# Mean and variance of six blocks: column sums in groups of 32 on VectorE, one 16-column product each on TensorE

## Chip, cores and metric

The kernel runs on one core of a Trainium2 chip. The metric is the time of one execution in microseconds (us), as the median of several; lower is better.

## What is computed

Eight batches go through an attention between 512 tokens and 32 states (8 heads of 64), then both results, joined to 544 rows of 512 channels, go through a normalised feed-forward layer and a gated convolution. What matters here is the normalisation in the middle:

```python
mu = np.mean(x, axis=-1, keepdims=True)
var = np.mean((x - mu) ** 2, axis=-1, keepdims=True)
xn = (x - mu) / np.sqrt(var + 1e-06) * g_ln
ch = np.maximum(xn @ w_ch1, 0.0) @ w_ch2
return (x + ch).astype(np.float32)
```

x has 512 channels (DM), w_ch1 maps them to 2048 (DFF), w_ch2 maps them back. The mean and the variance are sums over channels, one number for each token.

## The kernel before

Activations lie channels on partitions, tokens along the free axis: a block is the 512 tokens of one batch, held as four tiles of 128x512. So a sum over channels is a sum over partitions, and one number per token is wanted on all 128 partitions.

Matrix products with fp32 accuracy are made from two halves (type F32R), high and low: `mm3` (lines 77, 78, 79) issues three products for one. `segment(b, ...)` runs the feed-forward layer of block b in 16 steps f. In each step TensorE makes h, the hidden tile (6 products of 512 columns, lines 77 to 79 into the PSUM tag `mm`, which has two buffers), ScalarE and VectorE turn h into the halves `hid` (lines 680 and 684), and TensorE adds the step before into four accumulators (`second`, 12 products into `acc0` to `acc3`). The order of TensorE's instructions is the order in which the program writes them (`manual_schedule`); all other engines run each its own queue, filled by a planner from priorities (`at_prio`, a smaller number goes first) and the planner's own estimate of times.

The mean of blocks 2 to 7 is worked out ahead of the activations, from the attention weights `aT`: `mean_terms` makes a tile t of 128x512 in step 10 of the block before (lines 359, 360), `halves_of` splits it in two (lines 318, 320), and `x1_mean`, called in step 1 behind the products of h, lets `column_total` (line 327) multiply both halves with a matrix of ones, 512 columns each. That puts the mean (with a minus sign) of every token on every partition, in a PSUM buffer of the tag `at`. Just ahead of h in this step stand `m_steps` (line 144, small products of tile form 64*32) and `x1_group` (line 347, form 32*64), whose four results are copied from the accumulators' buffers to `x1` by ScalarE and VectorE (lines 354, 352).

The variance is made by the generator `x1_var`: four adds of x1 and the mean (line 375), squares on ScalarE (376), three adds on GpSimd (378, 381), `halves_of` again, and three steps later, at the end of step 4, `rstd_of`: `column_total`, a transposition of the 128x512 result in groups of 32 (line 333), a scale and offset on one column of each group (line 335, 128x16) and a power of -0.5 on GpSimd (line 337). `rstd_row` (line 430) transposes that back to a row after step 15, when the accumulators are scaled and added to x1 (lines 711, 714).

`background(b)` runs x1_var and then `attention_steps(b + 1)`, one piece a step. The last piece but one, in step 12, is `sread` (line 304, 32 products of tile form 128*32 into a buffer of the tag `mm`, then a transposition on VectorE, line 308). Step 13 begins with `m_steps` of the next block.

`t2` is a ring of six 128x512 buffers that all these steps share. Blocks 0 and 1 use another path (`x1_steps`), which also calls `halves_of` and `rstd_of`.

Of the kernel before, what the change touches and what calls it, by code (L numbers as in the profile page):

```python
# [9 lines left out]
F32 = mybir.dt.float32  # L10
# [10 lines left out]
P = 128  # L21
# [20 lines left out]


@with_exitstack
def tile_kernel(ctx: ExitStack, tc: tile.TileContext, xT, xk, stT, sn, w1, w2, wval, wout, convw, gln, ident, out):
    nc = tc.nc
    main = ctx.enter_context(tc.tile_pool(name="main", bufs=1))
    ps_acc = ctx.enter_context(tc.tile_pool(name="ps_acc", bufs=1, space=PSUM))
# [6 lines left out]
    def sb(shape, dt, tag, bufs=1):  # L55
        cnt[0] += 1
        return main.tile(shape, dt, tag=tag, bufs=BUFS.get(tag, bufs), name=f"{tag}_{cnt[0]}")
# [5 lines left out]
    def at_ps(shape):  # L63
        return ps(ps_at, "at", shape)
# [4 lines left out]
    def small(shape, dt, tag):  # L69
        return sb(shape, dt, tag, 2)  # L70
# [10 lines left out]
    def at_prio(p):  # L81
        tc.cur_priority = p

    x2d = [dram.tile([P, KT, S], F32, name=f"x2d{b}") for b in range(B)]
    x1d = dram.tile([B, P, KT, NS], F32, name="x1d")
    ident_sb = sb([P, P], F32, "ident")
    g_sb = sb([P, KT, 1], F32, "g")
    cw_sb = sb([P, KT, TAPS], F32, "cw")
    nhalf = sb([P, S // 32], F32, "nhalf")
# [19 lines left out]
    def load_xk(b):  # L109
        xn = sb([P, 4, H, D], F32, "big")  # L110
        nc.sync.dma_start(out=xn, in_=xk[b])
        loads[b].append(xn)
# [183 lines left out]
    def sread(b):  # L296
        a2T = a2s.pop(b)
        xn = loads[b][3]
        sr = ps(ps_mm, "mm", [P, 2, D]) if b > 1 else at_ps([P, 2, D])
        for u in range(2):  # L300
            for c in range(4):
                for p in range(KT):
                    r = slice(32 * p, 32 * p + 32)
                    nc.tensor.matmul(
                        sr[r, u, :], lhsT=a2T[u][:, c, r], rhs=xn[:, c, 2 * p + u, :], start=(c == 0), stop=(c == 3)
                    )
        srs = t2([P, 4, 32])
        nc.vector.transpose(srs.rearrange("p t n -> p (t n)"), sr.rearrange("p u d -> p (u d)"))
        for p in range(KT):
            nc.sync.dma_start(  # L310
                out=x1d[b, :, p, :].rearrange("(t j) n -> j t n", j=32), in_=srs[32 * p:32 * p + 32]
            )
# [3 lines left out]
    def halves_of(x, n, scale=1.0):  # L316
        hi, lo = (sb([P, n], F32R, "t2") for _ in range(2))
        nc.scalar.activation(hi, x, AF.Copy, scale=scale)
        if scale == 1.0:
            nc.gpsimd.tensor_tensor(lo, x, hi.bitcast(F32), op=ALU.subtract)  # L320
        else:
            nc.vector.scalar_tensor_tensor(lo, x, scale, hi.bitcast(F32), op0=ALU.mult, op1=ALU.subtract)
        return hi, lo

    def column_total(out, hl):
        for i in range(2):
            nc.tensor.matmul(out, lhsT=ones.to_broadcast([P, P]), rhs=hl[i], start=i == 0, stop=i == 1)

    def rstd_of(key, hl, n):
        var = ps(ps_mm, "mm", [P, n]) if key < 2 else at_ps([P, n])  # L330
        column_total(var, hl)
        turned = t2([P, n // 32, 32])
        nc.vector.transpose(turned.rearrange("p g n -> p (g n)"), var)
        rstd = small([P, n // 32, 1], F32, "rstd")
        nc.vector.tensor_scalar(rstd, turned[:, :, :1], 1.0 / DM, 1e-6, op0=ALU.mult, op1=ALU.add)
        rv = rstd.rearrange("p c o -> p (c o)")
        nc.gpsimd.tensor_tensor(rv, rv, nhalf[:, :n // 32], op=ALU.pow)
        rstds[key] = rstd

    def x1_group(b):  # L340
        sn_raw, aT = coef[b][1], aTs[b]
        x1s[b] = x1 = sb([P, KT, S], F32, "x1")
        xp = [ps(ps_acc, f"acc{k}", [P, S]) for k in range(KT)]
        for k in range(KT):
            r = slice(32 * k, 32 * k + 32)
            for u in range(2):
                nc.tensor.matmul(
                    xp[k][64 * u:64 * u + 64, :], lhsT=sn_raw[r, u, :], rhs=aT[r, u, :], start=True, stop=True
                )
        for k in range(KT):  # L350
            if k % 2:
                nc.vector.tensor_copy(x1[:, k], xp[k])
            else:
                nc.scalar.copy(x1[:, k], xp[k])

    def mean_terms(b):
        sbn, aT = coef[b][2], aTs[b]
        t = t2([P, S])
        nc.scalar.activation(t, aT[:, 0], AF.Copy, scale=sbn[:, 0])
        nc.vector.scalar_tensor_tensor(t, aT[:, 1], sbn[:, 1], t, op0=ALU.mult, op1=ALU.add)  # L360
        terms[b] = halves_of(t, S)

    terms = {}

    def x1_mean(b):
        mus[b] = mu = at_ps([P, S])
        column_total(mu, terms.pop(b))

    mus = {}

    def x1_var(b):
        x1, mu, sqs = x1s[b], mus[b], []
        for k in range(KT):
            xc = t2([P, S])
            nc.vector.tensor_tensor(xc, x1[:, k], mu, op=ALU.add)
            nc.scalar.activation(xc, xc, AF.Square)
            if k % 2:
                nc.gpsimd.tensor_tensor(sqs[-1], sqs[-1], xc, op=ALU.add)
            else:
                sqs.append(xc)  # L380
        nc.gpsimd.tensor_tensor(sqs[0], sqs[0], sqs.pop(), op=ALU.add)
        hl = halves_of(sqs[0], S)
        yield
        yield
        yield
        rstd_of(b, hl, S)
        yield

    def x1_steps(b):
        _, sn_raw, _, sbhl = coef[b]  # L390
# [42 lines left out]
    def attention_steps(b):  # L433
        state_coefs(b)
        sc = [at_ps([P, S]) for _ in range(2)]
        scores(b, sc)
        softmax2_exp(b, sc)
        yield
        softmax1_max(b)
        yield  # L440
        softmax2_norm(b)
        yield
        softmax1_norm(b)
        yield
        softmax2_turn(b)
        yield
        softmax1_out(b)
        mean_terms(b)
        yield
        yield  # L450
        sread(b)
        yield
        if b + 1 < B:
            load_state(b + 1)
            load_x(b + 1)
            load_xk(b + 1)
# [3 lines left out]
    def sread_block_steps():  # L460
        xs = sb([P, KT, NTS], F32, "big")
        for k in range(KT):
            nc.sync.dma_start(out=xs[:, k].rearrange("p (b n) -> p b n", n=NS), in_=x1d[:, :, k, :].rearrange("b p n -> p b n"))
        yield
        t = t2([P, 2, NTS])
        nc.gpsimd.tensor_tensor(t, xs[:, :2], xs[:, 2:], op=ALU.add)
        nc.gpsimd.tensor_tensor(t[:, 0], t[:, 0], t[:, 1], op=ALU.add)
        hl = halves_of(t[:, 0], NTS, -1.0 / DM)
        yield
        yield  # L470
        mu = at_ps([P, NTS])
        column_total(mu, hl)
        xc = sb([P, KT, NTS], F32, "big")
        xn = sb([P, 2, KT, NTS], F32R, "ahl")
        for k in range(KT):
            nc.vector.tensor_tensor(xc[:, k], xs[:, k], mu, op=ALU.add)
        yield
        for k in range(KT):
            nc.scalar.activation(xn[:, 0, k], xc[:, k], AF.Copy, scale=g_sb[:, k])
            nc.vector.scalar_tensor_tensor(  # L480
                xn[:, 1, k], xc[:, k], g_sb[:, k], xn[:, 0, k].bitcast(F32), op0=ALU.mult, op1=ALU.subtract
            )
        xns[B] = xn
        x1s[B] = xs
        yield
        sq = [t2([P, 2, NTS]) for _ in range(2)]
        for i in range(2):
            nc.scalar.activation(sq[i], xc[:, 2 * i:2 * i + 2], AF.Square)
        nc.gpsimd.tensor_tensor(sq[0], sq[0], sq[1], op=ALU.add)
        nc.gpsimd.tensor_tensor(sq[0][:, 0], sq[0][:, 0], sq[0][:, 1], op=ALU.add)  # L490
        hl = halves_of(sq[0][:, 0], NTS)
        yield
        yield
        rstd_of(B, hl, NTS)
        yield

# [118 lines left out]
    def segment(b, f0, f1, n, nxt, bg):  # L615
        accs = {}
        for f in range(f0, f1):
# [24 lines left out]
                    split_w1(f // 2 + 1)  # L642
            if f == 1 and 1 < b < B:
                x1_group(b)
            at_prio(base)
            h = ps(ps_mm, "mm", [P, n])
            if b < B:
# [21 lines left out]
            if unit == (1, 0) and f % QF == 2:  # L669
                at_prio(base - 1500)  # L670
                m_steps(*unit)
            if f == 1 and 1 < b < B:
                x1_mean(b)
            if f == f1 - 1:
                at_prio(base + LATE)
                for _ in bg:
# [193 lines left out]
    for o in order[8:20]:  # L870
        load_tile(*o)
    load_xk(1)
    for o in order[24:26] + order[20:24]:
        load_tile(*o)
    late = order[26:]
# [77 lines left out]
    def background(b):  # L953
        yield
        if b == 3:
            val_weights.append(prep_weights(wval, wv, ["raw"] * KT))
        for i, _ in enumerate(x1_var(b)):
            if i == 2 and val_weights:
                next(val_weights[0], None)
            yield  # L960
        if b + 1 < B:
            yield from attention_steps(b + 1)
        else:
            yield
            yield from sread_block_steps()

    def before_phase_b():
# [115 lines left out]
```

## Time and profile before

| what | value |
|---|---|
| median of 3 runs | 890.83 us (890.58 to 890.91) |
| the profiled execution | 890.99 us |
| its span, first to last instruction | 889.2 us |
| mean granted TensorE clock | 0.996 |
| TensorE busy | 873.5 us, 98% of the span |
| VectorE, ScalarE, GpSimd busy | 571.8, 385.8, 210.3 us |

The profile page gives busy time by engine, by slice of the span and by source line; the trace behind it gives every instruction with its start and duration. A product's recorded duration includes the way through the array, so the distance between the starts of two products says what one costs, not its duration.

### The profile page before, as it was taken

The page shows a single profiled execution, that of the slowest core. Times are in us where ns is not written, and L with a number is a line of the kernel's source. Part 1 is how long each engine was busy: PE and PEld are TensorE (multiplying, and loading weights), DVE is VectorE, ACT ScalarE, POOL GpSimd, SP SyncE. Part 2 cuts the span into 40 slices and gives each one's busy share as a digit, 9 for nine tenths or more (in the row PEclk, how much of TensorE's full clock was granted, in tenths as well). Part 3 has the DMA queues.
Part 4 walks back from the last instruction along what each step waited for, and adds up shares of the span by engine and source line. Part 5 has one row for each costly group of instructions (what it writes and reads, how often), then busy time and mean ns, then how long its engine had stood idle before and what let it go on. Part 6 is the DMA issues. An engine that isn't in the chain of part 4 may idle for free.

```text
span 889.2 us, 12522 instructions
## 1 busy us (share of the span) xinstructions
PE 873.5 (98%) x4970; PEld 666.0 (75%) x4970; DVE 571.8 (64%) x957; ACT 385.8 (43%) x715; POOL 210.3 (24%) x172
## 2 busy tenths in 40 slices
PE   7997999999999999999999999999999999999998
PEld 2355767777777777777777777777899988888886
DVE  6899985666644553573464446243468799988870
ACT  4865744243433341443443235132337555455531
POOL 0001010013234321513522442162301124322100
PEclk8999999999999999999999999999999999999999
DMA  9932210121112101211120100110130212222112
GB/s 358 408 109 74 98 52 1 74 73 53 51 48 76 54 0 52 74 51 52 51 71 1 63 36 1 27 48 1 48 139 6 95 71 77 90 96 95 69 73 72
DMA packets 26667, 66.44 MB, mean 75 GB/s; under 512 B 10864, under 2 KB 13040, under 8 KB 22512
## 3 DMA queue, kind: packets, MB, share of 16 engines
q1 hardware_dynamic: 25984, 65.24, 20.4%
q8 instruction: 39, 0.64, 0.3%
q10 hardware_dynamic: 624, 0.40, 0.2%
q14 instruction: 20, 0.16, 0.1%
HBM read 47.80 MB, written 17.83 MB: 74 GB/s over the span
## 4 chain that ended last, share of the span: by engine, by line
PE 92%; DVE 4%; DMA 2%; ACT 1%; issue 1%; SPq 0%; DVEq 0%; ACTq 0%
PE acc L77 16%; PE acc L78 16%; PE acc L79 16%; PE mm L77 9%; PE mm L78 9%; PE mm L79 9%; PE at L144 2%; PE at L77 2%; PE at L79 2%; PE at L78 2%; PE mm L144 1%; PE mm L982 1%; DMA big<-in_xT 1%; PE mm L651 1%; PE acc L697 1%; PE at L287 1%
## 5 line engine op out<-in xcount | busy, mean ns | idle before, releaser
L77 PE MATMUL acc<-hid,w 128*128 128x512 f32 (+1 forms) x560 | 212.3, 379 | 0.1
L78 PE MATMUL acc<-hid,w 128*128 128x512 f32 (+1 forms) x560 | 211.4, 378 | 0.0
L79 PE MATMUL acc<-hid,w 128*128 128x512 f32 (+1 forms) x560 | 211.3, 377 | 0.0
L684 DVE SCALAR_TENSOR_TENSOR hid<-mm,hid 128x512 fp32r<-128x512 f32 (+1 forms) x140 | 91.8, 655 | 159.5 <-ACT hid L680 159.4
L680 ACT ACTIVATE hid<-mm 128x512 fp32r<-128x512 f32 (+2 forms) x144 | 82.2, 571 | 205.5 <-PE mm L79 204.1
L77 PE MATMUL mm<-ahl,m 128*128 128x512 f32 (+1 forms) x312 | 119.7, 384 | 3.4 <-DVE ahl L249 1.7
L77 PEld LDWEIGHTS acc<-hid,w 128*128 128x128 f32 x560 | 105.4, 188 | 23.0 <-issue 1.7
L79 PEld LDWEIGHTS acc<-hid,w 128*128 128x128 f32 x560 | 105.4, 188 | 19.8
L78 PEld LDWEIGHTS acc<-hid,w 128*128 128x128 f32 x560 | 105.4, 188 | 19.5
L78 PE MATMUL mm<-ahl,m 128*128 128x512 f32 (+1 forms) x312 | 115.3, 369 | 1.2 <-DVE m L74 1.2
L79 PE MATMUL mm<-ahl,m 128*128 128x512 f32 (+1 forms) x312 | 115.0, 369 | 0.0
L763 DVE SCALAR_TENSOR_TENSOR ahl<-big,cw,ahl 128x511 f32<-128x511 f32 (+3 forms) x128 | 102.2, 843 | 0.3
L74 POOL TENSOR_TENSOR m<-mb,m 128x512 fp32r<-128x512 f32 x48 | 61.4, 1299 | 123.0 <-ACT m L73 123.0
L73 ACT ACTIVATE m<-mb 128x512 fp32r<-128x512 f32 x62 | 38.7, 632 | 110.7 <-DVE mb L155 110.5
L77 PEld LDWEIGHTS mm<-ahl,m 128*128 128x128 f32 x312 | 58.8, 188 | 36.7 <-issue 12.1
L78 PEld LDWEIGHTS mm<-ahl,m 128*128 128x128 f32 x312 | 58.9, 189 | 11.3 <-DVE m L74 2.4
L79 PEld LDWEIGHTS mm<-ahl,m 128*128 128x128 f32 x312 | 58.8, 189 | 9.9
L749 POOL TENSOR_TENSOR w<-big,w 128x512 fp32r<-128x512 f32 x24 | 38.1, 1617 | 92.8 <-ACT w L747 92.8
L78 PE MATMUL acc<-w,raw 128*128 128x512 f32 (+1 forms) x144 | 54.3, 377 | 0.0
L79 PE MATMUL acc<-w,raw 128*128 128x512 f32 (+1 forms) x144 | 54.3, 377 | 0.0
L77 PE MATMUL acc<-w,raw 128*128 128x512 f32 (+1 forms) x144 | 54.3, 377 | 0.0
L711 DVE TENSOR_TENSOR t<-acc,t 128x512 f32<-128x512 f32 (+1 forms) x44 | 28.0, 660 | 28.3 <-PE acc L79 28.2
(183 smaller groups left out, 1294.9 us busy)
## 6 DMA issues: line engine op xcount, KB each, us to landing
w<-in_w SPq DMA_DIRECT2D x20, 512.0 KB, 8.6
big<-in_xT SPq DMA_DIRECT2D x8, 1024.0 KB, 5.1
big<-in_xk SPq DMA_DIRECT2D x8, 1024.0 KB, 5.3
x2d<-x SPq DMA_DIRECT2D x8, 1024.0 KB, 4.0
big<-x2d SPq DMA_DIRECT2D x8, 1024.0 KB, 4.9
out<-hid SPq DMA_DIRECT2D x16, 512.0 KB, 2.8
raw<-in_w SPq DMA_DIRECT2D x12, 512.0 KB, 6.7
raw<-in_wval SPq DMA_DIRECT2D x4, 512.0 KB, 4.1
```

Of the source, the lines that this page charges most:

```text
L73: nc.scalar.activation(hi, src, AF.Copy)
L74: eng.tensor_tensor(lo, src, hi.bitcast(F32), op=ALU.subtract)
L77: nc.tensor.matmul(acc, lhsT=wh, rhs=xl, start=first, stop=False)
L78: nc.tensor.matmul(acc, lhsT=wl, rhs=xh, start=False, stop=False)
L79: nc.tensor.matmul(acc, lhsT=wh, rhs=xh, start=False, stop=last)
L144: nc.tensor.matmul(mp[u][32 * p:32 * p + 32, :], lhsT=stg[r, p, :], rhs=w1s[4 * q + p][r], start=True, stop=True)
L287: nc.tensor.transpose(tp[:, c, :], a2[u][:, c * P:(c + 1) * P], ident_sb)
L680: marks["act"] = nc.scalar.activation(hid[:, 0], h, AF.Relu)
L684: marks["dve"] = nc.vector.scalar_tensor_tensor(hid[:, 1], h, 0.0, hid[:, 0].bitcast(F32), op0=ALU.max, op1=ALU.subtract)
L711: marks["dve"] = nc.vector.tensor_tensor(t, accs[d], rrow, op=ALU.mult)
L749: nc.gpsimd.tensor_tensor(lo, src, hi.bitcast(F32), op=ALU.subtract)
L763: t = nc.vector.scalar_tensor_tensor(g[:, j:], x[:, :n - j], cw_sb[:, k, PAD - j:TAPS - j], g[:, j:], op0=ALU.mult, op1=ALU.add)
```

## The change

The sums inside each group of 32 partitions are made on VectorE. `token_parts` transposes a 128x512 tile in blocks of 32x32 and reduces the last axis, which leaves 128x16 numbers: partition 32g + j, column c holds the sum over the 32 channels of group g for token 32c + j. `token_totals` adds the four groups with one fp32 product: `stack`, a 128x128 matrix of 4x4 identities of size 32, times the 16 columns, so that all four groups hold the total.

For the mean, `x1_mean` copies the 128x16 totals out of PSUM and transposes them, broadcast, to a row of 128x512. It is called ahead of h in step 1, not behind it. For the variance the totals are in the form that line 335 wants, so the 128x512 transposition of line 333 falls away; the product moves from step 4 to step 12 of the block, behind `sread` of the next block (in block 7, which has no next block, to step 6). Both products write to the tag `mm` where `column_total` wrote to `at`. `stack` is one more input of 64 KB, loaded on SP's queue. The host makes it as `np.tile(np.eye(32), (4, 4))`.

```diff
+    def token_parts(x):
+        turned = t2([P, S // 32, 32])
+        nc.vector.transpose(turned.rearrange("p g n -> p (g n)"), x)
+        parts = small([P, S // 32], F32, "parts")
+        nc.vector.tensor_reduce(parts, turned, axis=AX.X, op=ALU.add)
+        return parts
+
+    def token_totals(parts):
+        total = ps(ps_mm, "mm", [P, S // 32, 1])
+        nc.tensor.matmul(total.rearrange("p g o -> p (g o)"), lhsT=stack_sb, rhs=parts, start=True, stop=True)
+        return total
+
+    def rstd_from(key, var, n):
         rstd = small([P, n // 32, 1], F32, "rstd")
-        nc.vector.tensor_scalar(rstd, turned[:, :, :1], 1.0 / DM, 1e-6, op0=ALU.mult, op1=ALU.add)
+        nc.vector.tensor_scalar(rstd, var, 1.0 / DM, 1e-6, op0=ALU.mult, op1=ALU.add)
...
-        terms[b] = halves_of(t, S)
+        terms[b] = token_parts(t)
...
     def x1_mean(b):
-        mus[b] = mu = at_ps([P, S])
-        column_total(mu, terms.pop(b))
+        total = token_totals(terms.pop(b))
+        means = small([P, S // 32, 1], F32, "means")
+        p = tc.cur_priority
+        at_prio(p - HLEAD)
+        nc.vector.tensor_copy(means, total)
+        at_prio(p)
+        row = t2([P, S // 32, 32])
+        nc.vector.transpose(row, means.to_broadcast([P, S // 32, 32]))
+        mus[b] = row.rearrange("p g n -> p (g n)")
...
-        hl = halves_of(sqs[0], S)
-        yield
-        yield
-        yield
-        rstd_of(b, hl, S)
-        yield
+        variances[b] = token_parts(sqs[0])
+        for _ in range(4):
+            yield
...
+    def x1_rstd(b):
+        rstd_from(b, token_totals(variances.pop(b)), S)
...
         sread(b)
+        if b > 2:
+            x1_rstd(b - 1)
...
             if f == 1 and 1 < b < B:
                 x1_group(b)
+                x1_mean(b)
             at_prio(base)
             h = ps(ps_mm, "mm", [P, n])
...
-            if f == 1 and 1 < b < B:
-                x1_mean(b)
...
     load_xk(1)
+    nc.sync.dma_start(out=stack_sb, in_=stack)
...
             yield
+            x1_rstd(b)
             yield from sread_block_steps()
```

## Rows read from the trace of the kernel before

**Rows 1.** The page: busy time by engine, and TensorE's granted clock in 40 slices

```profile
PE 873.5 (98%) x4970; PEld 666.0 (75%) x4970; DVE 571.8 (64%) x957; ACT 385.8 (43%) x715; POOL 210.3 (24%) x172
...
PEclk8999999999999999999999999999999999999999
```

**Rows 2.** Timeline of TensorE, block 3, steps 2 and 3: start, duration, line, operands

```profile
287.94 0.39 PE L77 MATMUL acc<-hid,w 128*128 128x512 f32 x1
...
290.67 0.39 PE L77 MATMUL mm<-ahl,m 128*128 128x512 f32 x1
...
292.02 0.39 PE L77 MATMUL acc<-hid,w 128*128 128x512 f32 x1
```

**Rows 3.** The same view, block 3, step 1: around the mean

```profile
280.73 1.20 PE L347 MATMUL acc<-aT,sn_raw 32*64 32x512 f32 x16
281.87 0.50 PE L77 MATMUL mm<-ahl,m 128*128 128x512 f32 x1
...
283.36 0.63 PE L327 MATMUL at<-t,ones 128*128 128x512 f32 x2
283.83 0.40 PE L77 MATMUL acc<-hid,w 128*128 128x512 f32 x1
```

**Rows 4.** The same view, block 3, from step 4 to 5: around the variance

```profile
298.82 0.63 PE L327 MATMUL at<-t,ones 128*128 128x512 f32 x2
299.29 0.39 PE L77 MATMUL mm<-ahl,m 128*128 128x512 f32 x1
```

**Rows 5.** Timeline of TensorE's weight loads, block 3, step 1

```profile
281.87 0.19 PEld L77 LDWEIGHTS mm<-ahl,m 128*128 128x128 f32 x1 [0.81 <-issue]
281.97 0.19 PEld L78 LDWEIGHTS mm<-ahl,m 128*128 128x128 f32 x1
```

**Rows 6.** Timeline of TensorE, block 1: eight fp32 transpositions, 128 columns each

```profile
99.24 1.04 PE L287 MATMUL at<-ident,t 128*128 128x128 f32 x8
100.03 0.48 PE L77 MATMUL mm<-ahl,m 128*128 128x512 f32 x1
```

**Rows 7.** Timeline of TensorE, block 2, from step 12 to 13

```profile
260.72 0.39 PE L79 MATMUL acc<-hid,w 128*128 128x512 f32 x1
261.04 1.10 PE L304 MATMUL mm<-big,t 128*32 128x64 f32 x64
262.07 1.09 PE L144 MATMUL at<-w,stg 64*32 64x512 f32 x16
263.09 0.50 PE L77 MATMUL mm<-ahl,m 128*128 128x512 f32 x1
```

**Rows 8.** Timeline of ScalarE, block 3: an x1 copy, the split of the squares

```profile
282.82 1.05 ACT L354 COPY x<-acc 128x512 f32<-128x512 f32 x2
...
291.12 0.63 ACT L318 ACTIVATE t<-t 128x512 fp32r<-128x512 f32 x1 [2.32 <-POOL t L381]
```

**Rows 9.** Timeline of weight loads, block 2, step 1

```profile
208.97 0.19 PEld L77 LDWEIGHTS acc<-hid,w 128*128 128x128 f32 x1 [0.46 <-DVE x L352]
```

**Rows 10.** VectorE's groups by form: form, count | busy us, mean ns | idle before

```profile
L233 DVE TENSOR_REDUCE mxden<-t 128x16 f32<-128x512 f32 x16 | 10.7, 672 | 0.0
...
L217 DVE STREAM_TRANSPOSE t<-at 128x512 f32<-128x512 f32 x14 | 9.2, 692 | 2.2 <-PE at L213 2.2
...
L335 DVE TENSOR_SCALAR rstd<-t 128x16 f32<-128x16 f32 x8 | 1.4, 174 | 0.2
```

**Rows 11.** Timeline of VectorE: sread's transposition in block 2, hid of step 2 in block 3

```profile
262.21 0.32 DVE L308 STREAM_TRANSPOSE t<-mm 128x128 f32<-128x128 f32 x1 [2.46 <-PE mm L304]
...
288.83 0.69 DVE L684 SCALAR_TENSOR_TENSOR hid<-mm,hid 128x512 fp32r<-128x512 f32 x1 [1.21 <-ACT hid L680]
```

**Rows 12.** Timeline of GpSimd, block 3: the last add of the squares

```profile
289.80 1.28 POOL L381 TENSOR_TENSOR t<-t,t 128x512 f32<-128x512 f32 x1
```

**Rows 13.** GpSimd's groups by form: the power

```profile
L337 POOL TENSOR_TENSOR rstd<-rstd,nhalf 128x16 f32<-128x16 f32 x8 | 23.4, 2930 | 59.7 <-DVE rstd L335 59.7
```

**Rows 14.** Timeline of SP's queue: an input of the size of stack

```profile
6.17 0.33 SPq L864 DMA_DIRECT2D ident<-in_ident  x1
```

More of the change, by code (lines that the diff above doesn't have):

```diff
@@ L44, in tile_kernel @@
 @with_exitstack
-def tile_kernel(ctx: ExitStack, tc: tile.TileContext, xT, xk, stT, sn, w1, w2, wval, wout, convw, gln, ident, out):
+def tile_kernel(ctx: ExitStack, tc: tile.TileContext, xT, xk, stT, sn, w1, w2, wval, wout, convw, gln, ident, stack, out):
     nc = tc.nc
@@ L86, in tile_kernel @@
     ident_sb = sb([P, P], F32, "ident")
+    stack_sb = sb([P, P], F32, "stack")
     g_sb = sb([P, KT, 1], F32, "g")
@@ L333, in rstd_of @@
         nc.vector.transpose(turned.rearrange("p g n -> p (g n)"), var)
+        rstd_from(key, turned[:, :, :1], n)
+    def token_parts(x):
[9 more added lines that the diff above has]
+    def rstd_from(key, var, n):
         rstd = small([P, n // 32, 1], F32, "rstd")
-        nc.vector.tensor_scalar(rstd, turned[:, :, :1], 1.0 / DM, 1e-6, op0=ALU.mult, op1=ALU.add)
+        nc.vector.tensor_scalar(rstd, var, 1.0 / DM, 1e-6, op0=ALU.mult, op1=ALU.add)
         rv = rstd.rearrange("p c o -> p (c o)")
@@ L381, in x1_var @@
         nc.gpsimd.tensor_tensor(sqs[0], sqs[0], sqs.pop(), op=ALU.add)
-        hl = halves_of(sqs[0], S)
-        yield
-        yield
-        yield
-        rstd_of(b, hl, S)
-        yield
+        variances[b] = token_parts(sqs[0])
+        for _ in range(4):
+            yield
+    variances = {}
+    def x1_rstd(b):
+        rstd_from(b, token_totals(variances.pop(b)), S)
     def x1_steps(b):
@@ L1069 @@
         "ident": np.eye(P, dtype=np.float32),
+        "stack": np.tile(np.eye(32, dtype=np.float32), (4, 4)),
     }
```

## Prediction

> **What bounds the kernel now.** I read the page's busy shares first, then the granted clock, then TensorE's timeline in the blocks that the change touches. TensorE is busy 98% of the span, VectorE 64%, GpSimd 24%, and TensorE runs at its upper level, 2.4 GHz, from the second slice on [rows 1]. Busy alone doesn't prove a bound, because recorded durations overlap; the starts do. Twelve products of 512 columns take 290.67 - 287.94 = 2.73 us, 0.227 us each, and the six of the next h take 292.02 - 290.67 = 1.35 us, 0.225 us each, with no gap at the change from one to the other [rows 2]. In blocks 3 to 7 this goes on for whole blocks. So there a product taken from TensorE gives back its 0.227 us, and work that goes to another engine costs nothing as long as it delays no product. The forecast is therefore a sum over TensorE, and the risks are waits.
>
> **What is removed.** Every mean and every variance has two products of 512 columns. Around the mean they take 283.83 - 283.36 = 0.47 us [rows 3], around the variance 299.29 - 298.82 = 0.47 us [rows 4]. Six blocks with one of each: 12 x 0.47 = 5.64 us.
>
> **What is added on TensorE.** Twelve fp32 products of 16 columns. An fp32 product runs as two passes: the 8 products of m_steps and the 32 of sread have 16 and 64 records [rows 7]. Each pass loads a 128x128 weight matrix, and with 16 columns there is too little to hide the load behind. No row shows that form. From below: the transpositions are eight passes with a full fp32 weight load and 128 columns, 100.03 - 99.24 = 0.79 us, 0.10 each [rows 6]; sread's 64 small passes take 262.07 - 261.04 = 1.03 us, four side by side, so 0.064 for four [rows 7]. I take 0.064 as the lower end of a pass. Where a load could not be hidden, the next one started 281.97 - 281.87 = 0.10 us behind it [rows 5]; the load's whole record is 0.19 us there, and that is the upper end. Two rows say 0.10 to 0.11 for a full load, so I take 0.11 a pass, 0.22 for one product.
>
> There is also a price for changing the tile form. Between the form 128*128 and sread's it shows as 261.04 - 260.72 = 0.32 us where a steady product takes 0.227: 0.09 [rows 7]. The mean's product stands between x1_group (form 32*64) and h (128*128), so that change is paid there now and later: nothing added. The variance's product stands between sread (128*32) and m_steps (64*32), two small forms, so one further change comes in, 0.09 us. Block 7's variance is alone between two full-form groups: none.
>
> So one mean gives back 0.47 - 0.22 = 0.25 us; one variance of blocks 2 to 6 gives 0.47 - 0.22 - 0.09 = 0.16, and that of block 7 0.25.
>
> The Trainium skill ("TensorEngine Tiling (Array Packing)", Key Properties) says that changing the tiling mode drains the engine; the 0.09 us is what the trace shows of it, and it speaks against putting the variance's product behind sread.
>
> **Block 2's mean.** There the products of step 1 already wait: the weight load at 208.97 was held 0.46 us by the x1 copy of line 352 [rows 9]. VectorE sets that moment, not TensorE, so what TensorE saves ahead of it is lost, and the new copy of 128x16 (0.17 us by the row of line 335 [rows 10]) may stand in front. I count 0, with -0.2 to +0.25 as ends.
>
> **Sum.** 5 x 0.25 + 0 + 5 x 0.16 + 0.25 = 1.25 + 0.80 + 0.25 = 2.3 us less.
>
> **What is hidden, and by what.** On VectorE each block gets two transpositions more (0.69 us each: three new ones, less line 333), two reductions (0.67 each) and a copy of 0.17: 2.9 us a block [rows 10], 17 us in all on an engine that idles a third of the time. It costs nothing unless hid is late: hid's second half of step 2 is done at 288.83 + 0.69 = 289.52 and is needed at 292.02 [rows 2, 11], so 2.5 us of cover; without it every further us costs one. ScalarE loses the two splits of 0.63 us [rows 8], GpSimd two subtractions; neither engine sets TensorE's pace, so no gain.
>
> The mean's row: means copy and transposition (0.17 + 0.69 us) stand on VectorE among line 352's copies and ahead of the adds of line 375. The copy waits for TensorE's total; behind it are queued the second x1 copy and hid of step 1. Both have more than a microsecond of cover. But the first accumulating product needs ScalarE's first x1 copy, done at about 282.82 + 0.53 = 283.35; it ran at 283.83 [rows 3, 8] and will come at about 283.58. Cover 0.23 us, so a cheaper total than mine gains at most that much again.
>
> The variance moved to step 12: its product takes one of the two `mm` buffers, so h of step 13 now needs sread's buffer, free after line 308's transposition, 262.21 + 0.32 = 262.53; h starts at 263.09 behind m_steps [rows 7, 11] and in the new kernel later still, so m_steps hides it by over 0.5 us; without it h would wait for that long. The power (2.93 us on GpSimd [rows 13]) now ends some 4 us after sread; queued behind it is the split of the next block's m, behind that only products two steps later, and rstd itself is needed after step 15, over 10 us on. In the scheduler's queue of VectorE the line 430 transposition may wait on the power ahead of a hid, 2.5 us of cover again. The load of `stack` is one issue more on SP's queue, 0.33 us as that of ident [rows 14]. What stands behind it are weights that are used much later; ends 0 to +0.3 us, I take 0. For m_steps, the totals and the freed `at` buffers I find no new wait.
>
> **Rivals.**
> (a) A short pass costs its whole weight load, 0.19 us: 0.38 for a product. Then a mean gives 0.09, a variance 0.00, block 7's 0.09: 5 x 0.09 + 0.09 = 0.54 us less, 890.3 on the median's scale. For: nothing of 16 columns covers a load. Against: the transpositions' 0.10 with records of 0.14 and 0.19 that overlap. "TensorE: Matmul & The Clock Gate" of the Trainium skill (Single matmul latency) puts an isolated product at (398 + N) / 2.4 ns, by my estimate 173 ns for 16 columns, which points this way; no row here has that form.
> (b) Slower: VectorE is blocked by GpSimd. The variance's token_parts reads the sum that GpSimd ends at 289.80 + 1.28 = 291.08 [rows 12]. If the planner puts transposition and reduction ahead of hid of step 2, hid waits: 291.08 + 0.69 + 0.67 + 0.69 = 293.13 against a need at 292.02, 1.1 us lost, in six blocks 6.6; with the 2.3 saved, 4.3 us slower, 895.1. It decides from the point where token_parts precedes that hid by more than the 2.5 us of cover. For: ScalarE was held 2.32 us by the same sum [rows 8], so the planner does misjudge GpSimd. Against: its split stood behind ScalarE's hid of that step, and VectorE's hid comes right after that.
> (c) Cheap passes: 0.064 each, 0.13 a product. A mean gives 0.34, a variance 0.25, block 7's 0.34, block 2's mean 0.25: 1.70 + 1.25 + 0.34 + 0.25 = 3.5 us less, 887.3.
> (d) The means are bound elsewhere, as in block 2: hid or the x1 copies are late by what was saved. Only the variances count: 1.05 us less, 889.8.
>
> **How the numbers follow.** The profiled execution took 890.99 us, 0.16 above the median of 890.83. 890.99 - 2.3 = 888.7, so 888.5 on the median's scale. Chances: the forecast (887.9 to 889.2) 0.48, (c) 0.20, (a) 0.14, (d) 0.10, (b) 0.08. Faster or slower means beyond 0.2%, 1.8 us, about what a measurement of this kernel can tell from no change: below 889.05 or above 892.6. The forecast lies below in nine of ten, (c) always, (a) and (d) are within: faster 0.64, same 0.28, slower 0.08. The range takes in (a) to (d) without (b) and the end of the unknown costs below: 886.8 to 890.6.
>
> **What would show it.** The distance from x1_group to h in step 1 should grow by 0.2 us and the accumulating products should follow h directly; from sread to m_steps it should grow by some 0.3; the period of a block, from one x1_group to the next, should shrink by 0.4 us. Hid waits on VectorE behind a transposition that waits for GpSimd would show (b); longer distances at the 16-column products would show (a). New gaps on TensorE anywhere else would make the prediction wrong.

## The result

The changed kernel takes 899.72 us in the median (898.13 to 900.32), beside 890.71 us of the kernel before. The medians differ by 9.0 us, 1.0%; the ratio on record is 1.0089, with a 95% interval of 1.0074 to 1.0104. It is slower, where 2.3 us less was forecast. The profiled execution took 899.56 us, with a span of 897.8.

The page's busy time by engine hardly differs from that of before [rows 1]:

```profile
PE 877.1 (98%) x4969; PEld 665.6 (74%) x4970; DVE 590.4 (66%) x987; ACT 377.6 (42%) x703; POOL 208.9 (23%) x160
```

VectorE has 18.6 us more, where 17 were forecast (part of it are longer adds, see below), and ScalarE and GpSimd have less. TensorE's 98% hides the loss again, because a waiting product doesn't lower it much. The waits of TensorE's weight loads from 200 to 620 us, blocks 2 to 7 (line waited for, total, times, longest), name it; the kernel before has no wait for `hid` in this stretch:

```profile
PEld acc L77 <- DVE hid L710: 12.5, 11, 1.5
```

**Where the time went.** I cut both traces at the first product of x1_group (line 347 before, 363 after) in each block. The start of block 2 is at 203.79 us before and at 205.01 after: 1.2 us are lost ahead of it, where only the load of `stack` and, from 197 us on, the column sums for block 2's mean are new. Blocks 2 to 6, to the start of block 7, take 378.71 us before and 385.92 after: 7.2 us. The rest takes 306.70 and 306.82. A block of steady work took 75.4 us and now takes 77.5 (blocks 3 and 4) or 76.4 to 76.7 (5 and 6).

Here is block 3 of the changed kernel, TensorE first (start, duration, line, operands, wait):

```profile
282.74 1.21 PE L363 MATMUL acc<-aT,sn_raw 32*64 32x512 f32 x16
283.87 0.40 PE L346 MATMUL mm<-parts,stack 128*128 128x16 f32 x2
284.12 0.48 PE L77 MATMUL mm<-ahl,m 128*128 128x512 f32 x1
...
285.59 0.43 PE L77 MATMUL acc<-hid,w 128*128 128x512 f32 x1
...
289.53 0.39 PE L79 MATMUL mm<-ahl,m 128*128 128x512 f32 x1
290.95 0.50 PE L77 MATMUL acc<-hid,w 128*128 128x512 f32 x1 [1.03 <-DVE hid L710]
...
294.93 0.39 PE L79 MATMUL mm<-ahl,m 128*128 128x512 f32 x1
296.10 0.50 PE L77 MATMUL acc<-hid,w 128*128 128x512 f32 x1 [0.78 <-DVE hid L710]
```

The 16-column product is cheap: from 283.87 to 284.12, two passes in 0.25 us. The accumulating products of step 1 are free to start when h is done (285.59), so nothing is lost at the place where the change was made. It is lost in steps 2 and 3: from 289.53 to 290.95 and from 294.93 to 296.10, where a product should follow in 0.23 us. That is 1.19 and 0.94 us. The product behind a wait lasts 0.34 us to the next one and not 0.23 (290.95 to 291.29), so each wait costs 0.11 us more. The first wait is there in all six blocks, 1.17 to 1.21 us each; the second is 0.94 in blocks 3 and 4, 0.2 in 2, 6 and 7, and nothing in 5. The eleven waits come to 9.6 us, and to 10.8 with the 0.11 behind each.

VectorE in the same block:

```profile
285.45 0.17 DVE L386 COPY means<-mm 128x16 f32<-128x16 f32 x1
285.65 0.71 DVE L389 STREAM_TRANSPOSE t<-means 128x512 f32<-128x512 f32 x1
286.49 3.73 DVE L398 TENSOR_TENSOR t<-x,t 128x512 f32<-128x512 f32 x4
290.20 0.69 DVE L710 SCALAR_TENSOR_TENSOR hid<-mm,hid 128x512 fp32r<-128x512 f32 x1
294.01 0.71 DVE L339 STREAM_TRANSPOSE t<-t 128x512 f32<-128x512 f32 x1 [3.12 <-POOL t L404]
294.76 0.69 DVE L341 TENSOR_REDUCE parts<-t 128x16 f32<-128x512 f32 x1
295.36 1.32 DVE L710 SCALAR_TENSOR_TENSOR hid<-mm,hid 128x512 fp32r<-128x512 f32 x2
```

Hid of step 1 (line 710) comes behind the four adds of x1 and the mean (line 398). In the kernel before it came ahead of them:

```profile
284.55 0.69 DVE L684 SCALAR_TENSOR_TENSOR hid<-mm,hid 128x512 fp32r<-128x512 f32 x1 [1.10 <-ACT hid L680]
285.16 2.47 DVE L375 TENSOR_TENSOR t<-x,at 128x512 f32<-128x512 f32 x4
```

And hid of step 2 comes behind the transposition and reduction of the squares, which wait 3.12 us for GpSimd. ScalarE's queue has the same order: two squares ahead of its half of hid of step 1.

```profile
287.35 0.63 ACT L399 ACTIVATE t<-t 128x512 f32<-128x512 f32 x1 [1.39 <-DVE t L398]
289.05 0.63 ACT L399 ACTIVATE t<-t 128x512 f32<-128x512 f32 x1 [1.07 <-DVE t L398]
289.59 0.58 ACT L706 ACTIVATE hid<-mm 128x512 fp32r<-128x512 f32 x1
```

h of step 1 had been done at about 285.8. ScalarE's half of hid ended at 290.17 and VectorE's adds at 290.22, so either queue made hid about equally late; no run parts the two. The four adds take 3.73 us, where the same adds took 2.47 with the mean in PSUM. VectorE's view by line shows how (count: shortest, median, longest in ns), first of the changed kernel, then of before:

```profile
L398 DVE TENSOR_TENSOR t<-x,t x24: 679/686/1780, 210.9 to 597.7; 128x512 f32<-128x512 f32 x24
```

```profile
L375 DVE TENSOR_TENSOR t<-x,at x24: 669/680/689, 210.0 to 588.2; 128x512 f32<-128x512 f32 x24
```

Most adds still take 0.68 us, but in each of blocks 3 to 7 one takes 1.78 and another 0.82 to 0.84. They are those that start while GpSimd works on the split of m (line 74):

```profile
285.48 2.99 POOL L74 TENSOR_TENSOR m<-mb,m 128x512 fp32r<-128x512 f32 x2
```

The long add starts at 287.24 and ends at 289.02, 0.55 us behind the end of GpSimd's second split (288.47). GpSimd's own instructions grow too: 2.99 us for two, where two took 2.54 before; it is the second that grew, which starts while the first add runs. The Trainium skill ("SBUF — State Buffer", SBUF: two separate sides) says that VectorE with two SBUF inputs and GpSimd share a pair of ports under an exclusive lock, held by the one that starts first for its whole instruction. These rows agree. With the mean in PSUM the add has one SBUF input, and the longest of 24 took 0.69 us. In block 2 the splits are done at 210.84, before the adds start, and the adds aren't slow:

```profile
210.94 2.50 DVE L398 TENSOR_TENSOR t<-x,t 128x512 f32<-128x512 f32 x4
```

Hid is late there all the same, by the order alone: VectorE's x1 copies end 5.0 us behind the start of x1_group in block 2 and 2.8 us behind it in block 3.

### The profile page after: what moved, and what is told of

Same layout as the page of the kernel before. It is cut to its first block, busy times and chain, and to the rows that moved or that the text cites. A ratio compares the mean times of both kernels' runs of the same rounds, so it can differ in the third digit from the quotient of the medians.

```text
span 897.8 us, 12501 instructions
## 1 busy us (share of the span) xinstructions
PE 877.1 (98%) x4969; PEld 665.6 (74%) x4970; DVE 590.4 (66%) x987; ACT 377.6 (42%) x703; POOL 208.9 (23%) x160
## 4 chain that ended last, share of the span: by engine, by line
PE 86%; DVE 9%; issue 2%; DMA 1%; ACT 1%; POOL 1%; DVEq 0%; ACTq 0%; SPq 0%
PE acc L77 16%; PE acc L78 16%; PE acc L79 16%; PE mm L77 9%; PE mm L78 8%; PE mm L79 8%; PE at L145 2%; PE at L77 2%; PE at L79 2%; PE at L78 2%; DVE t L398 2%; PE mm L145 1%; DVE mb L156 1%; PE mm L679 1%; PE at L288 1%
## 5 line engine op out<-in xcount | busy, mean ns | idle before, releaser
L789 DVE SCALAR_TENSOR_TENSOR ahl<-big,cw,ahl 128x511 f32<-128x511 f32 (+3 forms) x128 | 98.9, 822 | 0.3
L74 POOL TENSOR_TENSOR m<-mb,m 128x512 fp32r<-128x512 f32 x48 | 63.8, 1348 | 146.1 <-ACT m L73 146.0
L775 POOL TENSOR_TENSOR w<-big,w 128x512 fp32r<-128x512 f32 x24 | 45.9, 1946 | 83.0 <-ACT w L773 83.0
```

The lines of the kernel that those rows point to most:

```text
L74: eng.tensor_tensor(lo, src, hi.bitcast(F32), op=ALU.subtract)
L775: nc.gpsimd.tensor_tensor(lo, src, hi.bitcast(F32), op=ALU.subtract)
L789: t = nc.vector.scalar_tensor_tensor(g[:, j:], x[:, :n - j], cw_sb[:, k, PAD - j:TAPS - j], g[:, j:], op0=ALU.mult, op1=ALU.add)
```

## The experiments

Theory A: the product of the mean now stands ahead of h of step 1, so the mean is there earlier, and the planner, going by its own estimate of times, puts adds and squares ahead of hid of step 1. Rival B: VectorE is blocked by GpSimd's sum of squares (rival (b) of the prediction). Rival C: VectorE has too much to do in these steps, in whatever order. The kernel before had a median of 892.6 and 891.2 us in the two comparisons below, so the ratios are what to compare.

**The mean alone.** The variance is made as before.

```
-        variances[b] = token_parts(sqs[0])
-        for _ in range(4):
-            yield
+        hl = halves_of(sqs[0], S)
...
+        rstd_of(b, hl, S)
...
```

> The changed kernel with the variance made as before (split in halves, two products of 512 columns, in step 4); the mean as changed, ahead of h. Theory A (the mean's row is there before h of step 1, so the planner puts the four adds and the squares ahead of hid of step 1, and TensorE waits some 1.2 us in step 2 of each of six blocks): the wait stays, about 6 x 1.2 = 7.2 us, less six means at 0.24 saved = 1.4, so about 896.5 us. Rival B (VectorE is blocked by GpSimd's sum of squares, the rival (b) of the prediction, and is the main loss): that wait is gone with the old variance, so about 889.5 us.

Measured: 903.56 us, ratio 1.0125 (1.0108 to 1.0142). The wait stays, so B is not the main cause. It is even worse than expected, because step 3 waits too, 0.7 us in each block. There it is ScalarE that stands behind GpSimd, with the split of the squares (line 319) ahead of its half of hid:

```profile
294.97 0.63 ACT L319 ACTIVATE t<-t 128x512 fp32r<-128x512 f32 x1 [2.80 <-POOL t L404]
295.51 0.58 ACT L707 ACTIVATE hid<-mm 128x512 fp32r<-128x512 f32 x1
```

In the kernel before the same split stood behind hid of step 2 and cost nothing [rows 8]. So the second wait needs no token_parts: the adds, planned earlier, move the work on the squares ahead of the next hid.

**The variance alone.** The mean is made as before, behind h, in PSUM.

```
-        terms[b] = token_parts(t)
+        terms[b] = halves_of(t, S)
...
-        total = token_totals(terms.pop(b))
...
+        mus[b] = mu = at_ps([P, S])
+        column_total(mu, terms.pop(b))
```

> The changed kernel with the mean made as before (halves, two products of 512 columns behind h, result left in PSUM); the variance as changed. Theory A: hid of step 1 comes ahead of the adds again, nothing waits, the six variances save 5 x 0.14 + 0.24 = about 1 us: about 889.8 us. Rival B: the transposition and reduction of the squares still hold hid of step 2 behind GpSimd, 0.5 to 1 us in each block, so 893 to 896 us.

Measured: 889.25 us, ratio 0.9972 (0.9963 to 0.9981). No product waits for hid in blocks 2 to 7, and a block takes 75.27 us, 0.17 less than before, where 0.16 was forecast. VectorE waits for GpSimd here as well, but behind hid of step 2 and ahead of hid of step 3, where there is room:

```profile
290.50 0.69 DVE L704 SCALAR_TENSOR_TENSOR hid<-mm,hid 128x512 fp32r<-128x512 f32 x1 [1.34 <-ACT hid L700]
292.68 0.71 DVE L339 STREAM_TRANSPOSE t<-t 128x512 f32<-128x512 f32 x1 [1.48 <-POOL t L397]
293.42 0.69 DVE L341 TENSOR_REDUCE parts<-t 128x16 f32<-128x512 f32 x1
294.58 0.69 DVE L704 SCALAR_TENSOR_TENSOR hid<-mm,hid 128x512 fp32r<-128x512 f32 x1 [0.48 <-ACT hid L700]
```

**Hid first.** The changed kernel, with an order in the queues added and nothing else. The marks are set by the last hid.

```
-            nc.vector.tensor_tensor(xc, x1[:, k], mu, op=ALU.add)
-            nc.scalar.activation(xc, xc, AF.Square)
+            behind(nc.vector.tensor_tensor(xc, x1[:, k], mu, op=ALU.add), "dve")
+            behind(nc.scalar.activation(xc, xc, AF.Square), "act")
```

> The changed kernel with one thing added: the adds of x1_var are ordered behind VectorE's hid of step 1 and the squares behind ScalarE's, in the queues alone. Theory A: the waits of step 2 go, and with the adds later the transposition of the squares falls behind hid of step 2 too; what is left is the saving, some 2.2 us: about 888.6 us, or up to 1.3 more if the loss ahead of block 2 belongs to the change. Rival C (VectorE's longer work is the cause whatever the order: adds of 0.94 us and not 0.68, a transposition and a copy more): hid of step 2 stays late by about 1 us a block, 893 us or more.

Measured: 888.18 us, ratio 0.9957 (0.9943 to 0.9971): some 4 us faster than the kernel before. Rival C falls: VectorE does the same work, and the adds are still slow (3.30 us for four), but nobody waits for them. From the start of block 2 to the end this kernel takes 681.8 us and the changed one 692.7. The difference of 10.9 us is that of the eleven waits, 10.8, so the waits are the whole loss there.

```profile
285.82 0.69 DVE L710 SCALAR_TENSOR_TENSOR hid<-mm,hid 128x512 fp32r<-128x512 f32 x1
286.43 3.30 DVE L398 TENSOR_TENSOR t<-x,t 128x512 f32<-128x512 f32 x4
290.91 0.69 DVE L710 SCALAR_TENSOR_TENSOR hid<-mm,hid 128x512 fp32r<-128x512 f32 x1 [1.18 <-ACT hid L706]
293.52 0.71 DVE L339 STREAM_TRANSPOSE t<-t 128x512 f32<-128x512 f32 x1 [1.92 <-POOL t L404]
```

The transposition of the squares fell behind hid of step 2 by itself.

**The mean's product behind h.** Only its place in TensorE's order is put back.

```
                 x1_group(b)
-                x1_mean(b)
...
+            if f == 1 and 1 < b < B:
+                x1_mean(b)
             if f == f1 - 1:
```

> The changed kernel with the mean's product moved back behind h of step 1, where the products of 512 columns stood; all else as changed. Theory A: the row is late enough that the planner puts hid of step 1 first, so the waits go as with an order given by hand: about 888.6 us, up to 1.3 more if the loss ahead of block 2 belongs to the change. If the place of the product is not the cause: 897 to 900 us.

Measured: 888.10 us, ratio 0.9954 (0.9939 to 0.9970), the same as with the order by hand. h of step 1 comes 0.25 us earlier than with the product ahead of it, and the mean one h later. That moves hid to the front of VectorE's queue:

```profile
285.24 0.65 DVE L711 SCALAR_TENSOR_TENSOR hid<-mm,hid 128x512 fp32r<-128x512 f32 x1
285.81 3.29 DVE L398 TENSOR_TENSOR t<-x,t 128x512 f32<-128x512 f32 x4
```

**The row in PSUM.** Order and place of the mean are as changed, but the adds read it from PSUM.

```
-        row = t2([P, S // 32, 32])
+        row = at_ps([P, S // 32, 32])
```

> The changed kernel with the mean's row written to PSUM and not to SBUF, so that the four adds have one operand in PSUM as before the change; place and queue order of the mean as changed. Theory A with lock (the adds stand ahead of hid of step 1, and what makes hid late is that an add with both operands in SBUF that starts during a GpSimd instruction lasts until that ends: 1.78 us where the others take 0.68): the adds take 0.68 each again, hid of step 1 is some 1.2 us earlier, the wait in step 2 falls from 1.2 to 0.0-0.3 us a block: 891 to 894 us. If the order alone is the cause: the wait stays at 1.0 us or more, 897 us or more.

Measured: 892.66 us, ratio 1.0016 (1.0007 to 1.0026). The four adds take 2.48 us again and hid of step 1 is done in time, though it still stands behind them:

```profile
285.30 2.48 DVE L398 TENSOR_TENSOR t<-x,at 128x512 f32<-128x512 f32 x4
287.77 0.69 DVE L710 SCALAR_TENSOR_TENSOR hid<-mm,hid 128x512 fp32r<-128x512 f32 x1
291.55 0.71 DVE L339 STREAM_TRANSPOSE t<-t 128x512 f32<-128x512 f32 x1 [3.08 <-POOL t L404]
```

The wait of step 2 is gone in blocks 3 to 7, so there it needs both: the wrong order and the adds made long beside GpSimd's splits. Block 2 keeps its 1.17 us: its adds were not slow in the changed kernel either (2.50 us, and 2.48 here), and the late x1 copies leave the order alone enough to make hid late. The wait of step 3 stays, 0.9 us in blocks 3 and 4.

**The squares' transposition later.** In the changed kernel, only token_parts of the squares is queued behind hid of step 3.

```
-        variances[b] = token_parts(sqs[0])
-        for _ in range(4):
-            yield
+        yield
+        yield
+        variances[b] = token_parts(sqs[0], "dve")
+        yield
+        yield
...
```

> The changed kernel with one thing added: transposition and reduction of the squares are queued behind VectorE's hid of step 3; the adds stay ahead of hid of step 1. If the two waits are separate: the wait of step 2 stays (6 x 1.2 us), that of step 3 (2.4 us in all) goes: about 897 us. If the second wait only hands on the first: both stay, 899 us. If the squares' transposition were the main cause (rival (b) of the prediction): below 893 us.

Measured: 895.46 us, ratio 1.0050 (1.0033 to 1.0067). The waits are separate: that of step 3 is gone, that of step 2 is 1.14 to 1.22 us in each of the six blocks. This is the part of rival (b) in the loss, 2.4 us of waits in the changed kernel's trace against 7.2 of the first kind.

**The load of stack alone**, in the kernel before, read by nothing.

```
...
     load_xk(1)
+    nc.sync.dma_start(out=stack_sb, in_=stack)
...
```

> The kernel before with only the load of the 64 KB of stack added on SP's queue; nothing reads it. If the 1.2 us that the changed kernel lost ahead of block 2 come from the load: 891.9 us or more against the kernel before on this chip. If they come from the granted clock, which was at 0.5 for some 3 us around 73 and 87 us in the one profile and not in the other: no difference beyond the spread of the kernel before.

Measured: 891.90 us, ratio 1.0003 (0.9993 to 1.0012): no difference. The 1.2 us ahead of block 2 are not the load. They go with the granted clock, in the view of stretches (start and end, length, busy time and count of PE, PEld, DVE, ACT, POOL, then clock, DMA share, GB/s). The changed kernel:

```profile
60.00:75.00 15.00, 13.39 (x122) 9.03 (x121) 15.00 (x33) 9.63 (x20) 2.90 (x1) 0.89 0.22 79
75.00:90.00 15.00, 13.29 (x67) 8.53 (x69) 13.12 (x25) 6.93 (x12) 0.00 (x0) 0.89 0.21 61
```

The kernel before:

```profile
60.00:75.00 15.00, 12.89 (x125) 8.49 (x123) 15.00 (x33) 10.07 (x20) 2.90 (x1) 1.00 0.22 71
75.00:90.00 15.00, 12.16 (x70) 7.59 (x71) 13.19 (x24) 7.20 (x14) 0.00 (x0) 1.00 0.21 67
```

Some products at 71 to 75 and 85 to 88 us ran at 1.2 GHz, 0.427 us each and not 0.227, after TensorE had waited 1.6 us each for a ScalarE copy (line 292) and for mb (line 156); the kernel before has the same waits and no dip. The stack-only kernel, the row in PSUM and the later transposition show a clock of 1.00 there; the mean alone and hid first show the dip in both stretches, the variance alone, the mean behind h and the last run below in the second only. In the four traces without a dip block 2 starts at 203.6 to 204.2 us, in the six with one at 205.0 to 206.1. The kernel before spreads from 890.5 to 893.0 us in the second comparison. Two of the four without a dip (the row in PSUM, the later transposition) carry the change, so the change alone doesn't bring it. Why the changed kernel had it in its profiled execution is open.

**The variance's product back at step 4**, with the mean's behind h: a version built from what the runs showed.

```
-        variances[b] = token_parts(sqs[0])
-        for _ in range(4):
-            yield
+        parts = token_parts(sqs[0])
+        yield
+        yield
+        yield
+        rstd_from(b, token_totals(parts), S)
+        yield
...
```

> The changed kernel with the mean's product behind h of step 1 (as in the fourth run) and the variance's product where the two of 512 columns stood, behind step 4, between two groups of the full tile form. By the rows (two changes of tile form avoided) the variance's product costs 0.21 and not 0.32 us there, in five blocks 0.5 us: some 0.5 us less than the fourth run, a block of 74.97 us and not 75.08. If the power or line 430 waits in a bad place then, the same time as the fourth run or more.

Measured: 887.45 us, ratio 0.9956 (0.9941 to 0.9971). A block takes 74.95 to 75.05 us where the run with the mean behind h had 75.03 to 75.10, 0.08 us less a block in the mean, where 0.1 was expected. Whole times don't tell the two apart, but both beat the kernel before and the changed one. The product there costs as much as between full-form products anywhere:

```profile
299.57 0.29 PE L346 MATMUL mm<-parts,stack 128*128 128x16 f32 x2
299.71 0.48 PE L77 MATMUL mm<-ahl,m 128*128 128x512 f32 x1
300.02 0.40 PE L78 MATMUL mm<-ahl,m 128*128 128x512 f32 x1
```

From 299.57 to 300.02 are 0.45 us for the two passes and one product of 0.23: 0.22.

## Why the prediction was wrong

**What bounds the kernel** was right: TensorE's order, product behind product, and waits as the only risk.

**The sum over TensorE** was right in its terms. A 16-column product was put at 0.22 us; the mean's took 0.25, and h's six products behind it 1.47 (284.12 to 285.59) where they took 1.49 straight behind the small form [rows 3], so 0.23 net. The variance's behind sread was put at 0.31: from the last product ahead of sread to h it is 2.70 us now (262.39 to 265.09) and was 2.37 [rows 7], 0.33. The steady block of the kernels without waits (hid first, mean behind h) is 75.07 us against 75.44: 0.37 us less, against 0.41 forecast. The variance alone gave 0.17 of it, so the mean gives 0.20 where 0.25 was forecast. Rivals (a) and (c), dear and cheap passes, both fall, and so does (d), by which the means give nothing.

```profile
262.39 0.39 PE L79 MATMUL acc<-hid,w 128*128 128x512 f32 x1
262.71 1.10 PE L305 MATMUL mm<-big,t 128*32 128x64 f32 x64
263.74 0.40 PE L346 MATMUL mm<-parts,stack 128*128 128x16 f32 x2
264.07 1.09 PE L145 MATMUL at<-w,stg 64*32 64x512 f32 x16
265.09 0.50 PE L77 MATMUL mm<-ahl,m 128*128 128x512 f32 x1
```

**Two gains were missed.** The sum was 2.3 us; without the waits 3.6 to 3.8 are gained from block 2 on (685.4 us before, 681.8 with hid first, 681.6 with the mean behind h). In block 7 step 5 begins with m_steps, and its products waited for the `at` buffer that the variance's sum held. The kernel before, then hid first:

```profile
601.13 1.94 PE L144 MATMUL at<-w,stg 64*32 64x512 f32 x16
```

```profile
600.33 1.09 PE L145 MATMUL at<-w,stg 64*32 64x512 f32 x16
```

That is 0.85 us. The text said of the freed `at` buffers that it found no new wait; it did not look for an old one that would go. Block 2 is the other: from its x1_group to that of block 3 it took 76.94 us and takes 76.01 with hid first, 0.93 less where 0.16 was counted. VectorE's queue at the start of that block changed order. In the kernel before, one add to x with both operands in SBUF started 0.44 us into GpSimd's split of m (206.47 to 207.77) and took 1.41 us; with hid first the same adds take 0.68, so the x1 copy that holds the accumulating products ends 0.74 us sooner behind the start of x1_group. The kernel before, then hid first:

```profile
206.91 1.41 DVE L714 TENSOR_TENSOR x<-t,x 128x512 f32<-128x512 f32 x1
```

```profile
207.91 1.28 DVE L740 TENSOR_TENSOR x<-t,x 128x512 f32<-128x512 f32 x2
```

The prediction took the moment that VectorE sets there as fixed.

**The step that failed** is the one under "What is hidden": "behind it are queued the second x1 copy and hid of step 1. Both have more than a microsecond of cover." It listed the row's copy and transposition, 0.9 us, as what may stand ahead of hid of step 1, and not the four adds of line 375, which take the row. But what had kept the adds behind hid of step 1 was only that the mean came from a product behind h. With the product ahead of h this tie was cut, and the planner was free to put all four adds and two squares first; hid came at 290.20 and its product 1.19 us late. The second half of the same failure is the adds' duration: the prediction gave it no change, though one operand moved from PSUM to SBUF, in a stretch in which GpSimd splits m. In blocks 3 to 7 four adds at 0.60 apart would have fitted into the cover (the row in PSUM shows it); at 3.73 us they did not. In block 2 even adds of 0.68 did not fit.

**Rival (b)** was right as a mechanism and wrong in size and place. The transposition of the squares did hold hid of step 2 behind GpSimd, 0.94 us in two blocks (1.1 forecast for each) and 0.2 in three. It did so only where the adds had been planned early; with hid first it does not, as the argument against it said. Its chance of 0.08 was the only one given to a slower kernel, and it named the wrong wait.

**The load of stack**, put at 0 with an end of 0.3 us, cost nothing that can be measured. The x1 copies in block 2 still make its accumulating products wait, as forecast (0.32 us where 0.19 was before).

## What to carry to other kernels

When a producer is moved ahead of an instruction on one in-order engine, ask what its consumers were waiting for: that wait may be the only thing that kept them behind the critical instruction on the other engines, and a planner with its own times will fill the gap. Give such an order by hand, or leave the producer where it was; here either turned 1% slower into 0.4% faster. And when an operand moves from PSUM to SBUF, its VectorE instruction's duration must be read again, beside what GpSimd does in the same stretch.

## What the runs showed of the hardware

An add of 128x512 with both operands in SBUF takes 0.68 us, but 1.78 us where it starts 0.5 us into a GpSimd split: it ends 0.55 us behind the split. With one operand in PSUM the longest of 24 took 0.69, with the same splits beside it. GpSimd in turn took 1.75 us for a split that starts during such an add, where the one before it took 1.29.

A product of 128x128 fp32 weights with 16 columns costs TensorE 0.22 to 0.25 us in two passes, half of what two products of 512 columns cost (0.47). 0.11 to 0.12 us a pass is close to the 0.10 at which the next load followed one that could not be hidden [rows 5], so what is paid seems to be the load and not the columns; no run changed the columns alone.
